# Batch 0's K in whole runs on 64 partitions, a third wide PSUM tile at the start, and attention-times-V visits in two parts, in an attention and gated-FFN kernel on one Trainium2 core

## The chip, the cores and the metric

The kernel runs on one core of one Trainium2 chip (trn2). The metric is the device time of one execution in microseconds (us); lower is better. Before the change the runs gave 460.41 us in the median of 3 (460.27 to 460.72).

## The reference

The attention has no softmax: scores are scaled, cut at zero, squared and divided by the sequence length. Its output, heads side by side, is the input of a gated feed-forward layer with an RMS norm ahead of it.

```python
# q, k, v: (8 batches, 12 heads, 448 positions, 64), float32
scores = (1 / sqrt(64)) * q @ k.T
attn   = maximum(scores, 0) ** 2 / 448
x      = heads_side_by_side(attn @ v)          # (8 * 448, 768)
xn     = x / sqrt(mean(x * x) + 1e-6) * rms_g
g, val = xn @ w_gate, xn @ w_val               # (3584, 1536) each
out    = (g * sigmoid(g) * val) @ w_out        # (3584, 768), float32
```

## The kernel before, in words

**The order of the work.** The program is written out by a planner that runs while the kernel is built (class `Planner`, L62). Every piece of work is an `Op` with a cost in us per engine, with operations it depends on, a rank, and sometimes a due time; the planner keeps a clock for each engine, picks the next piece and emits its instructions. No scheduler reorders them afterwards, so an engine executes in exactly this order, and waits on semaphores in order. The costs are numbers in the source (for example 0.14 + n x 0.000833 us for a ScalarE eviction of n columns, L413). When TensorE has nothing to do for 0.3 us or more in the plan, `fill` (L955) emits matmuls of ones and zeros that no one reads (L966).

**Data.** Q, K and V are loaded by GpSimd's DMA queue and turned into bf16 on the way (L255, L269). Positions are dealt to partitions in runs: a head's K of 448 x 64 stands on 128 partitions as 4 chunks of 64 columns on partitions 0 to 63 and 3 chunks on partitions 64 to 127, so each K load is two DMAs, and a `memset` (L240) fills the missing chunk. For batches 0 and 1 TensorE transposes Q and K (L369: per pair of heads 8 matmuls of 128 columns for K and 8 of 112 for Q; VectorE copies the result to `qkT`, L379); later batches use DMA transposes (L293). The loads stand on GpSimd's queue in the order Q and K of batch 0 in three steps of 2, 4 and 6 heads (with the identity matrix for the transposes made after the first), V, the gate and value weights in slices, batch 1, the output weights.

**Attention**, per group of four heads (j = 0, 2, 4): score matmuls (`scores_full` L425, `scores_half` L443 for batch 0, which is worked in two halves of 224 queries), the "rest" chunk, i.e. the last 64 keys of both head pairs (L461), each into a wide PSUM tile of two banks (there are two); ScalarE or VectorE cuts at zero (`relu`, L405, L407), VectorE squares in place (L411). Then the AV visit (`attend`, L538) multiplies by V with 28 matmuls on quarters of the array, 64 rows by 64 columns each, four side by side. Rows 0 to 63 and rows 64 to 127 of the array add into the same PSUM rows one after the other: first 16 matmuls (low half for one pair of heads, high half for the other), then, after a wait for those to land (an empty instruction with a dependency, L537), 12 with the halves exchanged. ScalarE evicts the visit (L565).

**Feed-forward.** For the norm, squares are summed by a matmul with ones (`norm_sums`, L769); ScalarE takes ln and exp (L607, L611), VectorE scales (L616). The projections form a stream (class `Stream`, L635): each group accumulates in one single PSUM bank (four of them) over its K chunks, first with rows 0 to 63 (half 0), then with rows 64 to 127 (half 1); a step emits half 0 of one group beside half 1 of another. Before its half 1 a group keeps `APART` = 2 slots of distance (L725) and an empty instruction that waits for half 0 (L737). Groups marked `quarters` are emitted with outputs of 64 rows (tile 64 x 64, two matmuls per half), others with 128 (tile 64 x 128); `step` (L685) uses quarters when one of the pair asks for it.

Of the kernel before, what the change touches and what calls it, by code (L numbers as in the profile page):

```python
# [8 lines left out]
FP32 = mybir.dt.float32  # L9
# [5 lines left out]
U = 7  # L15
UH = 4
# [3 lines left out]
class Op:  # L20


    def __init__(self, on, fn, deps=(), rank=0, pair=None, bank=False, ends=None, due=None, ring=None,
                 early=0.0, lean=()):
        self.on, self.ring, self.early = on, ring, early
        self.fn, self.deps, self.rank = fn, list(deps), rank
        self.pair, self.bank, self.ends, self.due = pair, bank, ends, due
        self.done = NEVER
        self.lean = dict(lean)
        self.ps = None  # L30
# [31 lines left out]
class Planner:  # L62


    def __init__(self, banks):
        self.free = {"PE": 0.0, "ACT": 0.0, "DVE": 0.0, "POOL": 0.0, "SP": 0.0}
        self.lists = {e: [] for e in self.free}
        self.users = [[] for _ in range(banks)]
        self.stream = None
        self.fill = None  # L70
        self.now = 0.0

# [12 lines left out]
    def start(self, op, e, t):  # L85
        for x in op.on:
            self.lists[x].remove(op)
        dur = op.on[e]() if callable(op.on[e]) else op.on[e]
        self.free[e] = t + dur
        op.engine, op.begun = e, t  # L90
        op.done = op.ends(t) if op.ends else t + dur + (0.06 if e != "PE" else 0.22)
        op.fn(op)
# [67 lines left out]
def kernel(  # L160
# [11 lines left out]
    nc = tc.nc  # L172
# [22 lines left out]
    pairs = [psum.tile([P, 2, 512], FP32, name=f"psS{i}", tag=f"psS{i}") for i in range(2)]  # L195
    banks = [psum.tile([P, 512], FP32, name=f"psP{i}", tag=f"psP{i}") for i in range(4)]
    wide = [Space(pairs[i], (2 * i, 2 * i + 1)) for i in range(2)]
    single = [Space(banks[i], (4 + i,)) for i in range(4)]
# [44 lines left out]
    def load(nm, b, h0=0, h1=H, deps=()):  # L243
        runs = nm == "v" or b < PE_T
        src = src_of[nm][b, h0:h1]
        if nm == "q":
            parts = [(slice(0, PC), PC, 0, NCH)]
        else:
            parts = [(slice(0, D), D, 0, UH), (slice(D, P), D, UH if nm == "k" else UH - 1, U)]
        ops = []  # L250
        for prt, n, u0, u1 in parts:
            kb = n * (u1 - u0) * D * 4 * (h1 - h0) / 1e3

            def whole(prt=prt, n=n, u0=u0, u1=u1):
                nc.gpsimd.dma_start(  # L255
                    out=stage(nm, b)[prt, h0:h1, : (u1 - u0) * D],
                    in_=src.rearrange("h (p u) d -> p h (u d)", p=n)[:, :, u0 * D : u1 * D],
                )

            if runs:  # L260
                ops.append(pool_dma(0.72, kb, 400.0, whole, deps))
                continue
            step = u1 - u0 if nm == "q" else 1
            for u in range(u0, u1, step):

                def piece(prt=prt, n=n, u=u, u0=u0, step=step):
                    to = stage(nm, b)[prt].rearrange("p u (h d) -> p u h d", d=D)
                    rows = src.rearrange("h (p u) d -> p u h d", p=n)
                    nc.gpsimd.dma_start(  # L269
                        out=to[:, u - u0 : u - u0 + step, h0:h1, :], in_=rows[:, u : u + step]  # L270
                    )

                ops.append(
                    pool_dma(2.3 if step > 1 else 0.75, kb * step / (u1 - u0), 280.0, piece, deps)
                )
        landed.setdefault((nm, b), {}).update({h: ops for h in range(h0, h1)})
# [4 lines left out]
    turned = {}  # L281
# [72 lines left out]

    def blocks():
        return ((0, D), (D, P)) if state["quarters"] else ((0, P),)
# [3 lines left out]
    def transposes(b, j):  # L360
        def fn(op):
# [3 lines left out]
            op.flat = flat  # L365
            for nm, n, w, at in (("k", P, UH, 0), ("q", PC, NCH, S)):
                for c in range(w):
# [19 lines left out]
        t = Op({"PE": 0.55}, fn, need, rank=-2, bank=True)  # L387
        copy = Op({"DVE": 0.63}, copy_fn, [t], rank=0)
# [7 lines left out]
    def evict_rect(t, n, key, group):  # L396
# [12 lines left out]
        def square(op):  # L409
# [3 lines left out]
        rl = add(Op({"ACT": 0.14 + n * 0.833e-3, "DVE": 0.13 + n * 1.042e-3}, relu,  # L413
                    [t] + r_ring.before, rank=2, lean={"DVE": 0.9}))
# [4 lines left out]
    def scores_full(b, j, c, due):  # L419
# [13 lines left out]
        return add(Op({"PE": 0.19}, fn, [Turned(b, j)], rank=-1, pair=wide, due=due,  # L433
                      ring=r_ring, early=0.4))

    def scores_half(b, lo, what, due):

        def fn(op):
# [10 lines left out]
            for i, (j, c) in enumerate(what):  # L449
# [4 lines left out]
                      pair=wide, due=due,  # L454
# [11 lines left out]

    def rest(b, j, lo, w, due):
        def fn(op):
            emit_rest(op.ps.tile, b, j, lo, w)
            rl, sq = evict_rect(op, 2 * w, (b, lo, j, "rest"), (b, lo, j))  # L470
            rests[b, lo, j] = (sq, rl)
            plan.take(op.ps.banks, [rl])

        return add(Op({"PE": 0.25}, fn, [Turned(b, j), Turned(b, j + 1)], rank=-1,
                      pair=wide, due=due,
                      ring=r_ring, early=0.4))
# [29 lines left out]
    sqs, rests, avs = {}, {}, {}  # L506
    xTs, accs, attended, normed = {}, {}, {}, {}

    def attend(b, j, lo, w, due):
# [9 lines left out]
        def fn(op):  # L519
            ps = op.ps.tile  # L520
# [9 lines left out]
            last = {}  # L530
            for first in (True, False):
                for step in range(UH - (not first)):
                    for prt, jj in ((low, 0), (high, 1)) if first else ((low, 1), (high, 0)):
                        r, u = order[prt][jj][step]
                        for hh in range(2):
                            if not first and step == 0:
                                tc.add_manual_dep(nc.tensor.nop().ins, last[jj, hh].name, behind)  # L537
                            mm = nc.tensor.matmul(  # L538
                                out=ps[hh * D : (hh + 1) * D, jj, :w],
                                lhsT=vb[prt, 2 * (j + jj) + hh, u * D : (u + 1) * D],  # L540
                                rhs=r[prt, hh, :],
                                start=(first and step == 0),
                                stop=(not first and step == UH - 2),
                            )
                            last[jj, hh] = mm.ins
            ev = add(Op({"ACT": 0.14 + 2 * w * 0.833e-3}, evict, [op], rank=1))
# [39 lines left out]
        for jj in range(2):  # L586
            for i in range(UH - 1):
                need.append(Later(sqs, (b, j + jj, i) if full else (b, lo, j + jj, i)))
        need += [o for h in range(2 * j, 2 * j + 4) for o in landed["v", b][h]]
        me = Op({"PE": (1.55 if full else 0.9)}, fn, need, rank=-1,  # L590
                pair=wide, due=due)
        avs[b, lo, j] = me
# [8 lines left out]
    def norm_scale(b, lo, w, g):  # L601
# [11 lines left out]
        def scale(kt):  # L613
# [8 lines left out]
        rt = add(Op({"ACT": lambda: 2 * (0.19 + w * 0.833e-3) + switch(LN_EXP)}, root, [g.end],  # L622
# [3 lines left out]
            add(Op({"DVE": 0.2 + w * 1.05e-3}, scale(kt), [rt], rank=-1)) for kt in range(KT)  # L626
# [8 lines left out]
    class Stream:  # L635


        APART = 2
# [37 lines left out]
        def step(self, t):  # L676
# [8 lines left out]
            state["quarters"] = any(g.quarters for _, g in pair)  # L685
# [7 lines left out]
            took = max(g.slot for _, g in pair)  # L693
# [14 lines left out]
    class Group:  # L708
# [15 lines left out]
        def ready_at(self, half):  # L724
            t = self.when + stream.APART * self.slot if self.last not in (None, half) else 0.0  # L725
# [42 lines left out]

    def norm_sums(b, lo, w):  # L769
        if (b, lo) == (0, 0):  # L770
            return Group(
                KT, w, lambda i: ones_bf[:], lambda i: x2_bf[:, i, :],
                lambda g: norm_scale(b, lo, w, g), "psSS",
                lambda i: [Later(squared, i // 2 * 2)], False,
            )
# [3 lines left out]
            w == S,  # L779
# [4 lines left out]
    def silu(b, fb, lo, w):  # L784
        def done(g):
# [6 lines left out]
            op = add(Op({"ACT": lambda: 0.14 + w * 0.833e-3 + switch(SILU)}, fn, [g.end], rank=0,  # L792
# [6 lines left out]
    def hidden(b, fb, lo, w):  # L799
        def done(g):  # L800
# [8 lines left out]
            op = add(Op({"DVE": 0.15 + w * 1.042e-3}, fn, need, rank=1))  # L809
# [42 lines left out]
    def store(i, t, o, w, g):  # L852
# [15 lines left out]
        op = add(Op({"ACT": 0.14 + w * 0.833e-3, "DVE": 0.13 + w * 1.042e-3}, fn, [g.end] + ([] if first else [osts[i, t][2]]),  # L868
# [51 lines left out]
    def attention_half(lo):  # L920
        for j in range(0, HP, 2):
# [6 lines left out]
            rest(0, j, lo, HS, now)  # L928
            attend(0, j, lo, HS, now)

    def attention_full(b):
# [4 lines left out]
        for j in range(0, HP, 2):  # L936
# [3 lines left out]
            base = {0: 0.0, 2: 0.06, 4: 0.46}[j]  # L940
            if j == 0:
                for m in range(6):
                    scores_full(b, m // 3, m % 3, at("o", 0.15 + m * 0.12) if b > 2 else at("gv", 0.0))
                rest(b, 0, 0, S, at("gv", 0.0))
                attend(b, 0, 0, S, at("gv", 0.06))
                continue
            rest(b, j, 0, S, at("gv", base))
            for m in range(6):
                scores_full(b, j + m // 3, m % 3, at("gv", base + 0.02 + m * 0.06))
            attend(b, j, 0, S, at("gv", base + 0.4))  # L950
# [21 lines left out]
    pool_ident = add(Op({"POOL": 0.6}, lambda op: masks.make_identity(nc, ident[:])))  # L972
    load("q", 0, 2, 6)
    load("k", 0, 2, 6)
    load("q", 0, 6, 12)
# [13 lines left out]
    stream.add([norm_sums(0, 0, HS)])  # L989
    for b in range(B):  # L990
        groups = ffn(b)
        if b == 0:
            stream.add(groups[:24])
            plan.run(lambda: (0, 0) in summed)
# [61 lines left out]
```

## Time and profile before

| what | value |
|---|---|
| median of 3 runs | 460.41 us (460.27 to 460.72) |
| the profiled execution | 460.52 us, its span 458.7 us |
| first transposes / first AV visit / first projection | 7.59 / 18.00 / 30.42 us |
| first transposes of batch 1 | 48.16 us |
| start of the last matmul | 453.27 us |
| gate and value matmuls (L739, 64 x 448) | 349 ns each, four side by side |
| relu on ScalarE (L407), 128 x 896 | 908 ns |
| DMA moved | 44.75 MB, mean 98 GB/s |

How the views are read: the page has a line for each engine with its busy time and share of the span; PE is TensorE's matmuls, PEld its weight loads, which run beside them, DVE is VectorE, ACT ScalarE, POOL GpSimd. "PEclk" gives the granted TensorE clock in 40 slices, in tenths (9 is 90% or more). The chain of waits follows the work that ended last back to what released each step; "issue" is time for which nothing in the profile accounts. Rows of groups have the line, the engine, the operation, output<-input and the count, then busy time and mean length, then idle time before them and what ended it. A matmul's length in the records holds its pipeline, so the pace is read from starts.

### The profile page before, as it was taken

What the parts mean: (1) busy time and instruction counts of PE and PEld (TensorE: products, weight loads), DVE (VectorE), ACT (ScalarE), POOL (GpSimd) and SP (SyncE); (2) the same over time, 40 slices, a digit from 0 to 9 for tenths busy, and PEclk for the clock granted to TensorE, in tenths of its full rate; (3) what the DMA queues carried; (4) which work ended last, traced back from release to release, by engine and by line L of the source; (5) the groups of instructions that cost most, each with busy time, mean ns of one, the idle gap of its engine ahead of it and who ended that gap; (6) DMA issues with size and microseconds to landing.
All of it is one profiled execution on the core that took longest, in us unless ns stands there. A gap on an engine that the chain in (4) does not pass through costs nothing.

```text
span 458.7 us, 17067 instructions
## 1 busy us (share of the span) xinstructions
PE 447.9 (98%) x7829; PEld 338.9 (74%) x7829; DVE 243.6 (53%) x405; ACT 268.7 (59%) x394; POOL 78.4 (17%) x99
## 2 busy tenths in 40 slices
PE   8999999999899999999999999999999999999995
PEld 7668777777459777677769777677768777689974
DVE  1777786475645446636655347546655357522200
ACT  1685986485557565767647656667647657522221
POOL 8522711661061000700052000100000000000000
PEclk9999999999999999999999999999999999999999
DMA  9999999999969921994049920951002200021013
GB/s 103 198 204 200 203 181 150 139 185 160 136 78 168 137 74 27 142 195 59 1 62 171 143 80 20 143 102 37 3 2 64 65 16 3 1 79 29 1 37 103
DMA packets 130855, 44.75 MB, mean 98 GB/s; under 512 B 103008, under 2 KB 127200, under 8 KB 130784
## 3 DMA queue, kind: packets, MB, share of 16 engines
q0 software_dynamic: 91728, 24.39, 56.8%
q1 hardware_dynamic: 39056, 19.28, 24.4%
q8 instruction: 61, 1.00, 0.9%
q14 instruction: 10, 0.08, 0.1%
HBM read 48.76 MB, written 11.01 MB: 130 GB/s over the span
## 4 chain that ended last, share of the span: by engine, by line
PE 94%; DMA 2%; ACT 1%; POOL 1%; issue 1%; DVE 0%; ACTq 0%; POOLq 0%
PE psP L739 76%; PE psS L538 9%; PE psS L425 6%; DMA kb<-in_k_dram 2%; PE psS L461 1%; PE psP L966 1%; PE psS L443 1%; PE psP L369 1%; POOL kb L255 1%; ACT L343 1%; POOL qb L255 0%; ACT xT L565 0%; ACT r L407 0%; DVE xn L569 0%; ACT sil L789 0%
## 5 line engine op out<-in xcount | busy, mean ns | idle before, releaser
L739 PE MATMUL psP<-xn,wg_sb 64*64 64x448 bf16 (+1 forms) x2304 | 212.5, 338 | 1.6 <-issue 1.6
L739 PE MATMUL psP<-xn,wv_sb 64*64 64x448 bf16 (+1 forms) x2304 | 197.6, 338 | 0.1
L407 ACT ACTIVATE r<-psS 128x896 bf16<-128x896 f32 (+1 forms) x168 | 146.7, 908 | 55.5 <-PE psS L425 41.9
L739 PE MATMUL psP<-wo_sb,hT 64*128 64x384 bf16 (+1 forms) x1519 | 146.9, 324 | 0.0
L739 PEld LDWEIGHTS <-wg_sb 64*64 64x64 bf16 (+1 forms) x2304 | 123.7, 105 | 24.8 <-issue 3.8
L739 PEld LDWEIGHTS <-wv_sb 64*64 64x64 bf16 (+1 forms) x2304 | 121.2, 105 | 23.6 <-issue 4.0
L411 DVE TENSOR_TENSOR r<-r 128x896 bf16<-128x896 bf16 (+1 forms) x171 | 102.1, 613 | 67.6 <-ACT r L407 67.2
L739 PEld LDWEIGHTS <-hT 64*128 64x128 bf16 (+1 forms) x1519 | 103.1, 97 | 26.4 <-issue 9.7
L803 DVE TENSOR_TENSOR hT<-sil,psP 128x448 bf16<-128x448 bf16 (+1 forms) x108 | 61.2, 566 | 38.4 <-PE psP L739 37.9
L789 ACT ACTIVATE sil<-psP 128x448 bf16<-128x448 f32 (+1 forms) x108 | 54.0, 500 | 36.9 <-PE psP L739 36.3
L565 ACT ACTIVATE xT<-psS 128x896 bf16<-128x896 f32 (+1 forms) x27 | 22.5, 834 | 50.9 <-PE psS L538 50.9
L425 PE MATMUL psS<-qkT 64*64 64x448 bf16 (+1 forms) x412 | 48.2, 352 | 0.2 <-ACT r L407 0.2
L860 ACT COPY ost<-psP 128x384 f32<-128x384 f32 x55 | 26.4, 480 | 32.9 <-PE psP L739 32.7
L538 PE MATMUL psS<-r,vb 64*64 64x448 bf16 (+1 forms) x756 | 43.7, 333 | 1.9 <-PE psS L538 0.3
L255 POOL DMA_DIRECT2D vb<-in_v_dram x20 | 14.3, 728 | 166.2 <-PE psS L538 89.4
L616 DVE SCALAR_TENSOR_TENSOR xn<-xT,g_sb,rstd 128x448 bf16<-128x448 bf16 (+1 forms) x54 | 30.2, 627 | 15.2 <-ACT rstd L611 15.2
L269 POOL DMA_DIRECT2D kb<-in_k_dram x42 | 33.3, 1050 | 16.1 <-DMA wo_sb<-in_moe_w_out_dram 8.8
L538 PEld LDWEIGHTS <-vb 64*64 64x64 bf16 x756 | 22.2, 106 | 18.4 <-PE psS L538 11.2
L575 DVE TENSOR_TENSOR x<-xT 128x896 f32<-128x896 bf16 (+1 forms) x16 | 16.5, 1033 | 33.2 <-ACT xT L565 33.2
L425 PEld LDWEIGHTS <-qkT 64*64 64x64 bf16 (+1 forms) x412 | 20.3, 103 | 7.1 <-issue 2.9
L343 ACT ACT_TABLE_LOAD x18 | 23.1, 1283 | 1.0 <-PEq L1040 0.7
L575 DVE TENSOR_TENSOR acc<-xT 128x896 f32<-128x896 bf16 (+1 forms) x8 | 8.3, 1033 | 22.8 <-ACT xT L565 22.8
(37 smaller groups left out, 155.9 us busy)
## 6 DMA issues: line engine op xcount, KB each, us to landing
vb<-in_v_dram POOLq DMA_DIRECT2D x12, 384.0 KB, 7.5
kb<-in_k_dram POOLq DMA_DIRECT2D x43, 96.0 KB, 12.0
qb<-in_q_dram POOLq DMA_DIRECT2D x6, 672.0 KB, 15.4
out_dram<-ost SPq DMA_DIRECT2D x8, 336.0 KB, 3.1
wg_sb<-in_moe_w_gate_dram POOLq DMA_DIRECT2D x4, 576.0 KB, 15.2
wv_sb<-in_moe_w_val_dram POOLq DMA_DIRECT2D x4, 576.0 KB, 17.2
wo_sb<-in_moe_w_out_dram POOLq DMA_DIRECT2D x2, 1152.0 KB, 14.0
out_dram<-ost SPq DMA_DIRECT2D x8, 288.0 KB, 2.7
```

What stands on the lines that cost most here:

```text
L269: nc.gpsimd.dma_start(out=to[:, u - u0 : u - u0 + step, h0:h1, :], in_=rows[:, u : u + step])
L343: nc.scalar.add_instruction(mybir.InstLoadActFuncSet(name=name, act_func_set_id=n, ins=[], outs=[]))
L407: nc.scalar.activation(out=op.view, in_=src, func=ACT.Relu)
L411: eng.tensor_tensor(out=rl.view, in0=rl.view, in1=rl.view, op=ALU.mult)
L425: nc.tensor.matmul(out=ps[m0:m1, hh, :S], lhsT=qkT[b][prt, j, 0, c * P + m0 : c * P + m1], rhs=qkT[b][prt, j, 1, :], start=True, stop=True,)
L538: mm = nc.tensor.matmul(out=ps[hh * D : (hh + 1) * D, jj, :w], lhsT=vb[prt, 2 * (j + jj) + hh, u * D : (u + 1) * D], rhs=r[prt, hh, :], st ...
L575: nc.vector.tensor_tensor(out=dst, in0=x, in1=x, op=ALU.mult)
L616: nc.vector.scalar_tensor_tensor(out=xns[b][:, kt, lo : lo + w], in0=xTs[b][:, kt, lo : lo + w], scalar=g_sb[:, kt : kt + 1], in1=rstd[:, ...
L739: mm = nc.tensor.matmul(out=self.ps[m0:m1, : self.w], lhsT=self.lhsT(i)[prt, m0:m1], rhs=self.rhs(i)[prt], start=(half == 0 and i == 0), s ...
L789: nc.scalar.activation(out=s[:, :w], in_=g.ps[:, :w], func=ACT.Silu)
L803: nc.vector.tensor_tensor(out=hT[:, fb, o : o + w], in0=sil[b, fb, lo][1][:, :w], in1=g.ps[:, :w], op=ALU.mult,)
L860: nc.scalar.copy(out=to, in_=g.ps[:, :w])
```

## The change

Eight things change, all in the writing of the instruction list:

1. Batch 0's K is loaded with 7 positions a partition on 64 partitions, one DMA a load, into a part of the output weights' tile that is not yet used; its transposes are 14 matmuls of 64 columns on quarters. The identity is made after two loads of each.
2. Until the sums of batch 0's first half are done, four single banks are two, and a third wide tile stands in their place.
3. An AV visit becomes two operations, and the next group's rest chunk depends on the first of them having been issued, with rank -4 (ahead of the second, rank -3).
4. The planner knows a form for each TensorE operation and adds 0.12 us where it changes; the stream keeps quarters while a quarter group is open.
5. The norm's sums don't ask for quarters; those of the first half of batch 0 become three operations with whole 128-row matmuls.
6. A group's second half follows after max(slot, 0.2) us instead of two slots.
7. The planned costs and latencies of ScalarE, VectorE and TensorE operations are changed.
8. For batch 1, transposes use one single bank, and the order of rest and scores within a group is changed.

```diff
@@ Planner.start @@
         dur = op.on[e]() if callable(op.on[e]) else op.on[e]
+        if e == "PE":
+            dur += self.changed(op.form() if callable(op.form) else op.form)
         self.free[e] = t + dur
-        op.engine, op.begun = e, t
-        op.done = op.ends(t) if op.ends else t + dur + (0.06 if e != "PE" else 0.22)
+        op.engine, op.begun, op.left = e, t, t + dur
+        op.done = op.ends(t) if op.ends else t + dur + {"ACT": 0.17, "DVE": 0.13, "PE": 0.22}.get(e, 0.1)
...
+    wide = [bank_pair(psum, i) for i in range(2)]
+    single = [bank(psum, i) for i in (4, 5)]
+    head = tc.tile_pool(name="psum_head", bufs=1, space=bass.MemoryType.PSUM)
+    wide.append(bank_pair(head.__enter__(), 3))
+
+    def end_head():
+
+        wide.pop()
+        head.__exit__(None, None, None)
+        pool = ctx.enter_context(tc.tile_pool(name="psum_rest", bufs=1, space=bass.MemoryType.PSUM))
+        single.extend(bank(pool, i) for i in (6, 7))
@@ load @@
+        if (nm, b) == ("k", 0):
+
+            def runs_of_seven():
+                nc.gpsimd.dma_start(
+                    out=wo_sb[:D, h0:h1, :S], in_=src.rearrange("h (p u) d -> p h (u d)", p=D)
+                )
@@ transposes @@
+            for u in range(U if b == 0 else 0):
+                at = u * P if u < UH else (u - UH) * P + D
+                for hh in range(2):
+                    nc.tensor.transpose(
+                        out=flat[hh * D : (hh + 1) * D, at : at + D],
+                        in_=wo_sb[:D, 2 * j + hh, u * D : (u + 1) * D],
+                        identity=ident[:D, :D],
+                    )
@@ evict_rect @@
-        rl = add(Op({"ACT": 0.14 + n * 0.833e-3, "DVE": 0.13 + n * 1.042e-3}, relu,
-                    [t] + r_ring.before, rank=2, lean={"DVE": 0.9}))
+        rl = add(Op({"ACT": 0.05 + n * 0.833e-3, "DVE": 0.07 + n * 1.042e-3}, relu,
+                    [t] + r_ring.before, rank=2, lean={"DVE": 0.5 if key[:2] == (0, 0) else 3.0 if key[0] == 0 else 0.9}))
@@ rest @@
-        return add(Op({"PE": 0.25}, fn, [Turned(b, j), Turned(b, j + 1)], rank=-1,
-                      pair=wide, due=due,
-                      ring=r_ring, early=0.4))
+        need = [Turned(b, j), Turned(b, j + 1)] + ([Issued(ones[b, lo, j - 2])] if j else [])
+        return add(Op({"PE": 0.0025 + w / 2400.0}, fn, need, rank=-4 if j else -1,
+                      pair=wide, due=due, form="q", ring=r_ring, early=0.4))
@@ attend @@
+        def begin(op):
+            plan.take(op.ps.banks, [me])
+            products(True, op.ps.tile)
+
+        def fn(op):
+            op.ps = one.ps
+            products(False, op.ps.tile)
...
-        me = Op({"PE": (1.55 if full else 0.9)}, fn, need, rank=-1,
-                pair=wide, due=due)
-        avs[b, lo, j] = me
+        slot = w / 2400.0 + 0.0025
+        one = Op({"PE": UH * slot}, begin, need, rank=-1, pair=wide, due=due, form="q")
+        me = Op({"PE": (UH - 1) * slot}, fn, [one], rank=-3, form="q")
+        avs[b, lo, j], ones[b, lo, j] = me, one
+        add(one)
         return add(me)
@@ Stream.step, Group.ready_at @@
-            state["quarters"] = any(g.quarters for _, g in pair)
+            state["quarters"] = any(g.quarters for _, g in pair) or any(
+                g.quarters and g.count[0] for g in self.open
+            )
...
-            took = max(g.slot for _, g in pair)
+            took = max(g.slot for _, g in pair) + plan.changed(form())
...
-            t = self.when + stream.APART * self.slot if self.last not in (None, half) else 0.0
+            t = self.when + max(self.slot, 0.2) if self.last not in (None, half) else 0.0
@@ norm_sums (the first half of batch 0 has a class Sums of its own) @@
             lambda g: norm_scale(b, lo, w, g), "psSS", lambda i: [Later(summed, (b, lo))],
-            w == S,
+            False,
@@ the loads @@
     load("k", 0, 0, 2)
-    pool_ident = add(Op({"POOL": 0.6}, lambda op: masks.make_identity(nc, ident[:])))
     load("q", 0, 2, 6)
     load("k", 0, 2, 6)
+    made["ident"] = add(Op({"POOL": 0.6}, lambda op: masks.make_identity(nc, ident[:])))
```

## Prediction

> **What bounds the kernel now.** I read the page first (engine shares, clock, chain), then the chain of waits around one attention visit, the group row of that line, the timeline around changes of tile form, and the chain of the first 16 us.
>
> ```profile
> span 458.7 us, 17067 instructions
> PE 447.9 (98%) x7829; PEld 338.9 (74%) x7829; DVE 243.6 (53%) x405; ACT 268.7 (59%) x394; POOL 78.4 (17%) x99
> ...
> PEclk9999999999999999999999999999999999999999
> ...
> PE 94%; DMA 2%; ACT 1%; POOL 1%; issue 1%; DVE 0%; ACTq 0%; POOLq 0%
> ```
>
> TensorE is busy or holds the chain throughout, at full clock, while VectorE and ScalarE have 40% to spare. So the time is the length of TensorE's own instruction list, and the question is how much of that list is no work. The chain of waits from 181 to 187 us (start, length, what):
>
> ```profile
> 180.99 1.51 PE psP L739 x32
> 182.51 0.81 PE psS L538 x16
> 183.32 0.01 issue
> 183.33 0.79 PE psS L538 x12
> ```
>
> 32 gate/value matmuls of 448 columns, four side by side on quarters of the array, are 8 slots in 1.51 us: 0.189 us a slot. The attention-times-V visit (L538) has 28 matmuls, 7 slots, which should take 1.32 us; it takes 0.81 + 0.01 + 0.79 = 1.61. So 0.29 us a visit is a wait in its middle, where the second products (3 slots) may only start when the first (4 slots) have landed in the same PSUM rows. The group row of the line and a timeline around 13.5 us (start, length, engine, line, what):
>
> ```profile
> L538 PEld LDWEIGHTS <-vb 64*64 64x64 bf16 x756 | 22.2, 106 | 18.4 <-PE psS L538 11.2
> ```
> ```profile
> 12.59 0.94 PE L966 MATMUL psP<-busy_bf,ones_bf 128*128 128x224 bf16 x8
> 13.48 0.29 PE L461 MATMUL psS<-qkT 64*64 64x224 bf16 x4
> 13.70 0.36 PE L966 MATMUL psP<-busy_bf,ones_bf 128*128 128x224 bf16 x2
> ```
>
> The weight loads of L538 stood 11.2 us behind L538 itself. In the timeline, 8 fills of 224 columns are 8 x 0.096 = 0.77 us, yet the next form (64*64) starts 0.89 after the first of them; its one slot of 0.096 takes 0.22 until the form goes back. Each change of form costs **0.12 us**. The third loss is the head:
>
> ```profile
> 6.57 0.61 POOL kb L255
> 7.17 7.13 DMA kb<-in_k_dram
> 14.30 0.04 issue
> 14.35 1.46 PE psP L369 x48
> ```
>
> The third part of batch 0's K lands at 14.30; the first gate/value matmul follows at 30.42 (timeline), and 79 of the 120 fills (matmuls that do no work) stand between the first transposes (7.59) and it.
>
> **The change, part by part.** The built order of both kernels is known, so instructions can be counted; only waits are open.
>
> *AV visits split.* In the built order two slots (the next group's rest chunk and a gate/value slot, or two gate/value slots) stand between the 16 and the 12 of every visit of full width but the first, which has two transposes there, and the two beside half-width projections, which have more. Inside a visit now, the fifth slot starts 0.45 us after the fourth (0.189 of work, 0.26 of wait). With two slots between it is 0.57 after: no wait is left. 21 full visits x 0.29 = **-6.0 us**. Behind the waiting matmuls stands all of TensorE's list, so nothing else becomes late in exchange; the eviction of a visit (L565) comes 0.38 later, and the wide tile with it. The six half-width visits lose 6 x 0.28 = 1.7; of them one keeps its wait, one has a single slot of 0.096 in the gap (0.14 stays), four lose it for two further changes of form each, which the next part counts: **-1.3**.
>
> *Changes of form.* Counted in the built orders: 117 before, 86 after. Up to batch 1's first transposes they rise from 41 to 50, from there on they fall from 76 to 36 (per later batch from 8 to 2, since quarters are kept while such a group is open and the sum-of-squares group no longer asks for them). 31 x 0.12 = **-3.7**. At a change both halves of the array must be empty, and laid end to end by slots without waits the two lists differ by 3.7: 2.2 of that are 23 fewer fills (0.096 each), **-1.5** the rest, mostly halves that stood idle until the other had ended.
>
> [...]
>
> *New half-to-half waits.* The stream now lets a group's second half follow after one slot or 0.2 us, before after two. 224-column visits show 0.096 + 0.23 us needed from the last first-half matmul's start, 448-column ones 0.189 + 0.26; 384 columns show no such wait before, so I bound it by these two and take 0.25. In the built order 16 out-projection groups stand 0.32 apart and lack 0.095 each (1.5), the norm sums, six gate/value groups and some visits about 0.4 more: **+1.9** (bounds 0, if the wait is shorter there, and +3, if the 36 groups that stand 0.42 apart wait too).
>
> *Head.* By counts from the first transposes to the first gate/value matmul: fills 79 to 60 (-1.8), score visits 14 to 11 (3 x 0.19 = -0.6), one rest less (-0.1), K's transposes 14 of 64 columns (0.2 us) for 8 of 128 (0.22) (0), the norm sums in whole form without their half-to-half waits (-0.9), the waits of the three visits 0.85 to 0.4, one or two more changes (+0.2), K's wait of 0.28 + 0.15 at 14.3 gone: 22.83 becomes **18.6**, and with 4 fewer fills ahead of the first transposes (7.59 to 7.2) the projection starts at 25.8 instead of 30.4. ScalarE is the engine beside it (by the starts of its rows some 11 us of work in 18); the third wide tile lets it run three evictions behind. The single tiles that it takes away feed nothing there but transposes and fills.
>
> *To batch 1's transposes.* Before 17.74 us with 233 projection matmuls; after 258 (+1.2), 3 scores and a rest more (+0.7), 7 changes more (+0.8), visit waits -0.7: 19.7, so **45.5** instead of 48.16. Those transposes need batch 1's K: heads 0 to 5 landed at 47.9 (issued by GpSimd at 30.2, 17.7 us to landing). Nothing but the queue's order holds that, since DMA moves 198 to 204 GB/s from 11 to 57 us (page). What moves it is the start: GpSimd issues K in three DMAs instead of six, so the last K part goes out 3 x 0.61 = 1.8 us sooner; at the most the queue also loses its slack (1.4 MB of Q and K at 200 GB/s from 2.8 us would end at 9.7 and land near 10.1, 4.2 sooner). Between 1.8 and 4.2 I take 3.0, the middle: K of batch 1 at 44.9, just ahead of TensorE. At 1.8 it costs 0.6, at 0 2.4. The identity, now issued after two loads of each, is done by some 4.6 us, and the first transposes need it at 7.2; past it move one Q and one K load.
>
> [...] Each of the six K loads before already writes 64 partitions, and 11 to 14 us shows 184 to 202 GB/s with them. [...]
>
> *From there to the end.* Before 405.1 us (48.16 to 453.27, the last matmul's start). Visits -6.0, 40 changes fewer -4.8, new waits +1.9, 25 projection matmuls already done -1.2, idle halves -1.3; and a single stall of 1.6 us (with nothing shown that released it, at 123.2 in the timeline) may or may not be met again: -0.8. 405.1 becomes **392.9**. The planner's ScalarE and VectorE costs now are nearer to the starts in the trace (relus 0.81 apart), so I expect evictions on time.
>
> *Sum.* -0.4 (fills ahead) -4.2 (head) +2.0 (to batch 1) -12.2 = -14.8; I give back 0.6 for small waits of the new order: **-14.2**. The profiled execution took 460.52 (span 458.7 and 1.8 around it): 446.3. The median of the runs is 460.41, 0.1 less, so I say 446.2.
>
> **Rivals.**
> 1. *The transfers don't come sooner* (or K lands late on 64 partitions). Then TensorE stands before batch 1's transposes for the 2.4 us above: 448.6, and up to 3 more if K lands later than now; about 449. For it: DMA is saturated from 14 to 57 us. Against: the queue was underfed from 2 to 7 us (10 to 152 GB/s). Chance 0.16.
> 2. *The visits' wait moves.* With the rest chunk pulled between two visits, its eviction stands ahead of the visit's own, and the next score waits for a wide tile, of which two are left after the head. If each of the 21 full visits so returns its 0.29: 446.2 + 6 = 452. Against: ScalarE is 59% busy. Chance 0.13.
> 3. *Slower: evictions become the bound.* The planner now counts 0.80 us for a wide relu, 0.09 less than before; the records last 0.908. If the real pace were the record's length, each of the 168 evictions (L407) would free its tile 0.11 late and TensorE, in order, would stand: +18, 464. It decides from 0.085 us an eviction (14.2 / 168). Against: four relus stand in 2.97 us on ScalarE's timeline, closer than their lengths. Chance 0.04.
> 4. *The split does nothing* (the wait for the landing is ordered elsewhere): 446.2 + 7.3 = 453.5. Chance 0.02.
> 5. Better still (no new half waits, no stall): 442 to 444. Chance 0.05.
>
> **How the numbers follow.** The forecast has the remaining 0.60, with 443.5 to 449 as its own range. Cases 1 and 2 reach to 452, so the range is 442.5 to 452. A difference under 0.2% can't be told from none here. All cases but 3 are faster: 0.95; within 0.2% 0.01, slower 0.04.
>
> **What would show it.** Right: in the chain of waits the 12 of a visit follow other matmuls, and L538's idle row falls from 11.2 to about 2; the first gate/value matmul near 26, batch 1's first transposes near 45.5, and 361.77 to the last matmul (91.5 before) shorter by about 2. Wrong: score matmuls waiting for ScalarE, a DMA ahead of L369's successor, or out-projection rows with gaps of more than 0.1 us.

## The result and the profile after

The changed kernel took 455.42 us (median of 4 runs, 453.62 to 456.05), the kernel before 460.57 beside it (460.27 to 461.36): a ratio of 0.988, 95% interval 0.985 to 0.991. The direction was right, but 446.2 was forecast and the range ended at 452.0: of 14.2 us, 5.2 came. The profiled execution took 453.62, 7.3 over the 446.3 that the prediction's sum gave for it.

The page of the changed kernel (span; busy time of each engine, share, instructions; granted clock in 40 slices; the engines' shares of the chain that ended last):

```profile
span 451.9 us, 16996 instructions
...
PE 440.2 (97%) x7805; PEld 327.5 (72%) x7805; DVE 241.7 (53%) x403; ACT 268.8 (59%) x395; POOL 76.8 (17%) x96
...
PEclk9999999999899999999999999999999999999998
...
PE 88%; DMA 9%; issue 1%; POOL 1%; ACT 0%; ACTq 0%; POOLq 0%
```

TensorE still bounds the kernel, but a DMA now stands in the chain with 9% (2% before), and in the eleventh slice the clock was not full. In the changed kernel's source the projections stand at L802 (L739 before), the visits at L590 (L538), the scores at L468 (L425), the rest chunk at L504 (L461) and the transposes at L411 (L369), batch 0's K at L403. Three group rows, the first of the kernel before (busy, mean ns of one, then the idle time before them and what ended most of it):

```profile
L739 PE MATMUL psP<-xn,wg_sb 64*64 64x448 bf16 (+1 forms) x2304 | 212.5, 338 | 1.6 <-issue 1.6
...
L802 PE MATMUL psP<-xn,wv_sb 64*64 64x448 bf16 (+1 forms) x2304 | 204.6, 340 | 3.1 <-issue 3.1
...
L590 PEld LDWEIGHTS <-vb 64*64 64x64 bf16 x756 | 24.5, 106 | 10.0 <-issue 1.8
```

The 11.2 us that the AV line's weight loads stood behind their own matmuls are gone (the greatest reason left has 1.8), as predicted. The gate/value matmuls, however, now wait 3.1 us for nothing that the profile shows; before it was 1.6. The chain of waits around one visit shows the split at work (start, length, what):

```profile
108.68 0.76 PE psS L590 x16
109.44 0.19 PE psS L504 x4
109.63 0.19 PE psP L802 x4
109.82 0.57 PE psS L590 x12
```

16 and 12 matmuls now take 0.76 and 0.57, 1.33 us in all where the visit took 1.61, and two slots of other work stand between. So that step did what it should. The chain shows how; what the split is worth is measured below. Where the time went shows when TensorE's starts are set against the prediction. Visits are counted from 0, half-width ones too; A9 is the start of visit 9. The last column is the kernel "held" of the experiments, whose TensorE list is that of the changed kernel, matmul for matmul:

| start, us | before | predicted | after | held |
|---|---|---|---|---|
| batch 0's first transposes | 7.59 | 7.2 | 6.72 | 7.63 |
| first gate/value matmul | 30.42 | 25.8 | 26.64 | 26.92 |
| batch 1's first transposes | 48.16 | 45.5 | 46.77 | 46.76 |
| A9 | 102.58 | | 97.65 | 97.92 |
| A12 | 153.46 | | 151.19 | 147.44 |
| last matmul | 453.27 | 438.4 | 446.36 | 442.86 |

Up to A9 4.9 us are won; from A9 to A12 2.7 of them are lost again (50.88 before, 53.54 after, while held takes 49.52 for the same matmuls); behind A12 4.65 are won. The chain in the stretch:

```profile
117.02 2.13 PE psP L802 x39
119.16 1.71 issue
120.87 0.82 PE psP L802 x6
121.69 0.37 PE psS L468 x4
122.06 3.52 PE psP L802 x48
```

TensorE stands 1.71 us for no shown reason, and 1.2 us later 48 matmuls take 3.52 us, where the chain elsewhere has 48 in 2.33. The windows of the same stretch show why the second happens (the DMA share adds up the time of packets over that of 16 engines and passes 1 where packets overlap; it serves for comparison only):

```profile
core 0: us, PE busy (x) PEld busy (x) DVE busy (x) ACT busy (x) POOL busy (x), PEclk, DMA share, GB/s
118.00:120.00 2.00, 1.16 (x19) 0.49 (x18) 1.69 (x3) 0.85 (x2) 0.00 (x0) 1.00 1.97 81
120.00:122.00 2.00, 1.13 (x16) 0.94 (x19) 0.00 (x0) 0.28 (x1) 0.00 (x0) 0.76 2.58 129
122.00:124.00 2.00, 2.00 (x27) 1.11 (x23) 0.00 (x0) 1.08 (x2) 0.00 (x0) 0.50 3.78 131
```

The clock falls to half for 3.4 us after the stall (0.50 from 121.05 to 124.46). Two smaller stalls stand at 105.5 and 112.5, one at 209.9. The kernel before had a large one, the one that the prediction booked with -0.8, as something that "may or may not be met again"; the clock stayed full behind it (1.00 in every window from 122 to 130 us):

```profile
123.22 0.37 PE L739 MATMUL psP<-xn,wg_sb 64*64 64x448 bf16 x1 [1.59 <-issue]
```

### The profile page after: what moved, and what is told of

It reads as the page before. It is cut to its first block, busy times and chain, and to the rows that moved or that the text cites. A ratio compares the mean times of both kernels' runs of the same rounds, so it can differ in the third digit from the quotient of the medians.

```text
span 451.9 us, 16996 instructions
## 1 busy us (share of the span) xinstructions
PE 440.2 (97%) x7805; PEld 327.5 (72%) x7805; DVE 241.7 (53%) x403; ACT 268.8 (59%) x395; POOL 76.8 (17%) x96
## 4 chain that ended last, share of the span: by engine, by line
PE 88%; DMA 9%; issue 1%; POOL 1%; ACT 0%; ACTq 0%; POOLq 0%
PE psP L802 74%; PE psS L590 6%; PE psS L468 6%; DMA kb<-in_k_dram 4%; DMA wv_sb<-in_moe_w_val_dram 4%; DMA wo_sb<-in_k_dram 2%; PE psS L504 1%; PE psP L411 1%; POOL qb L286 0%; POOL wo_sb L270 0%; ACT ost L941 0%; POOL ident masks.py:199 0%; POOL ident masks.py:197 0%; ACTq L941 0%; POOLq L1126 0%
## 5 line engine op out<-in xcount | busy, mean ns | idle before, releaser
L802 PE MATMUL psP<-xn,wg_sb 64*64 64x448 bf16 (+1 forms) x2304 | 222.1, 340 | 0.0
L802 PE MATMUL psP<-xn,wv_sb 64*64 64x448 bf16 (+1 forms) x2304 | 204.6, 340 | 3.1 <-issue 3.1
L450 ACT ACTIVATE r<-psS 128x896 bf16<-128x896 f32 (+1 forms) x169 | 148.3, 913 | 47.3 <-PE psS L468 25.3
L802 PEld LDWEIGHTS <-wg_sb 64*64 64x64 bf16 (+1 forms) x2304 | 123.5, 105 | 39.8 <-PE psP L802 9.1
L802 PE MATMUL psP<-wo_sb,hT 64*128 64x384 bf16 (+1 forms) x1502 | 139.5, 323 | 0.0
L802 PEld LDWEIGHTS <-wv_sb 64*64 64x64 bf16 (+1 forms) x2304 | 118.0, 105 | 29.0 <-issue 4.3
L802 PEld LDWEIGHTS <-hT 64*128 64x128 bf16 (+1 forms) x1502 | 101.8, 97 | 22.7 <-issue 2.8
L468 PE MATMUL psS<-qkT 64*64 64x448 bf16 (+1 forms) x412 | 50.5, 352 | 0.0
L590 PE MATMUL psS<-r,vb 64*64 64x448 bf16 (+1 forms) x756 | 45.8, 331 | 0.1
L590 PEld LDWEIGHTS <-vb 64*64 64x64 bf16 x756 | 24.5, 106 | 10.0 <-issue 1.8
L468 PEld LDWEIGHTS <-qkT 64*64 64x64 bf16 (+1 forms) x412 | 21.7, 104 | 5.9
L637 DVE TENSOR_TENSOR acc<-acc,x 128x896 f32<-128x896 f32 (+1 forms) x16 | 16.5, 1033 | 0.6
## 6 DMA issues: line engine op xcount, KB each, us to landing
kb<-in_k_dram POOLq DMA_DIRECT2D x42, 96.0 KB, 14.2
```

What stands on the lines that cost most here:

```text
L450: nc.scalar.activation(out=op.view, in_=src, func=ACT.Relu)
L468: nc.tensor.matmul(out=ps[m0:m1, hh, :S], lhsT=qkT[b][prt, j, 0, c * P + m0 : c * P + m1], rhs=qkT[b][prt, j, 1, :], start=True, stop=True,)
L590: mm = nc.tensor.matmul(out=ps[hh * D : (hh + 1) * D, jj, :w], lhsT=vb[prt, 2 * (j + jj) + hh, u * D : (u + 1) * D], rhs=r[prt, hh, :], st ...
L802: mm = nc.tensor.matmul(out=self.ps[m0:m1, : self.w], lhsT=self.lhsT(i)[prt, m0:m1], rhs=self.rhs(i)[prt], start=(half == 0 and i == 0), s ...
```

## The experiments

**What the stalls are.** One count was made on the traces alone: TensorE's instructions (matmuls, weight loads and the few semaphore instructions that the profile lists) are numbered in the order of their starts, and for five numbers the table gives the largest gap in ns between two starts there. An ordinary gap at these places is 30 to 180.

| kernel | 3266 | 3522 | 3778 | 4034 | 4290 |
|---|---|---|---|---|---|
| before | 150 | 92 | 402 | 1941 | 162 |
| before_v_first | 150 | 92 | 152 | 150 | 146 |
| after | 152 | 709 | 1120 | 2058 | 178 |
| late | 151 | 1047 | 1120 | 2332 | 177 |
| whole | 632 | 609 | 1207 | 1943 | 146 |
| forms | 29 | 1164 | 1243 | 2491 | 1242 |
| apart2 | 404 | 1244 | 1095 | 1966 | 1668 |
| v_first | 180 | 985 | 297 | 156 | 177 |
| held | 439 | 436 | 120 | 90 | 374 |
| vf_apart2 | 150 | 30 | 230 | 92 | 93 |

The columns are 256 instructions apart. In kernels with different lists the large gaps fall on the same numbers, whatever the instruction there does, and later ones (7106 at 209.9 us in after) lie a multiple of 256 further. The five kernels not in the table agree: vf_whole, vf_forms and vf_kold have a gap of 618, 1068 and 1067 at 3522 (vf_forms another of 420 at 3778), vf_wide2 one of 1138 at 3778, and held_apart2 one of 874 at 9410, which is 21 x 256 behind 4034. One 16-KB packet of the DMA queue "instruction" comes for each such step (61 in the changed kernel's page, and TensorE's 15,632 listed instructions are 61 x 256 and 16 more). The reading that fits all this is that TensorE waits there for its own next block of instructions. In the changed kernel the packets for 3522, 3778 and 4034 begin when TensorE is 180, 204 and 214 instructions into the block before, where from 155 to 187 us, with little DMA (a share of 0.37 against 1.71 from 105 to 121), most begin within 60. The packets themselves take 0.97, 0.95 and 0.89 us, no longer than others (0.89 to 1.89 from 60 to 215 us): it is their start that is late, and the stalls end 2.3 to 3.3 us after it.

What moves there in the changed kernel: from 98 to 121 us the DMA transposes of batch 3's Q and K (256-byte packets); beside them up to 108 us batch 3's V (512-byte packets), and from 106 us on batch 4's Q and K (128-byte packets; issued from 97.1, but they stand behind V). So the gap at 3522, at 105 us, has only V beside the transposes; those at 3778 and 4034 have Q and K.

**v_first** and **before_v_first**: in the changed kernel and in the one before, from batch 4 on V is loaded ahead of Q and K. V's buffer comes free late, so that Q and K wait behind it on GpSimd's queue. TensorE's list is not touched.

```
+            if b >= 2:
+                load("v", b + 2, deps=last)
+                seen = last
             load("q", b + 2, deps=seen)
             load("k", b + 2, deps=seen)
-            load("v", b + 2, deps=last)
+            if b < 2:
+                load("v", b + 2, deps=last)
```

> The changed kernel with one edit: from batch 4 on, V is loaded ahead of Q and K, so that Q and K of batches 4 to 7 wait on GpSimd's queue behind V, which waits for an attention visit some 20 us later. TensorE's list is the same, instruction for instruction. Theory A (the stalls of 0.4, 0.8 and 1.7 us at 105, 112 and 119 us, and the half clock after the last, are TensorE waiting for its own instructions, which come by DMA and stand behind the small packets of batch 4's Q and K beside batch 3's transposes): the stalls go, the clock stays at 1.0 from 121 to 124 us, and the time falls by 3 to 5 us to 449 to 451. Theory B (they belong to this place of the list: an unlisted wait or a change of form): the same stalls stay at the same matmuls, time within 1 us of the changed kernel. Theory C (DMA traffic matters, but moves with the loads): the stalls go from 100 to 125 and come again some 20 us later, time within 2 us.

> The same edit in the kernel before, TensorE's list unchanged. Theory A: its one stall of 1.6 us at 121 to 123 us goes, 458 to 459. Theory B: it stays, 460.4. Theory C: a stall of about that size elsewhere.

Measured: 450.02 (448.66 to 450.92; 0.976 of before, 0.973 to 0.978) and 458.62 (457.79 to 459.13; 0.994, 0.992 to 0.996), beside 460.93 for the kernel before. TensorE's waits in v_first (us, times, longest):

```profile
PE psP L802 <- issue: 0.6, 1, 0.6
```

5.4 us come off the changed kernel by its median (3.3 in the profiled executions) and 2.3 off the one before; both times lie inside theory A's spans, and the gap at 4034 is gone in both. Theory A's other half did not hold for all: the gap at 3522 stays in v_first (985 ns), where V moves beside the transposes as before. With the loads moved in both, the change is worth 8.6 us and not 5.2.

**late** and **held** ask whether it helps that V goes first, or that the small packets move apart from the transposes. late keeps the order and gives the loads one more condition in the planner; held makes the wait a real one, on GpSimd, for the last transpose of the batch before (kept in `moved`).

```
# late
+            after = list(turned[b + 1]) if b >= PE_T else []
-            load("q", b + 2, deps=seen)
+            load("q", b + 2, deps=seen + after)
...
# held
+                def hold(op, b=b):
+                    tc.add_manual_dep(nc.gpsimd.nop().ins, moved[b + 1].ins.name, behind)
+                seen = [add(Op({"POOL": 0.1}, hold, seen + turned[b + 1]))]
             load("q", b + 2, deps=seen)
```

> The changed kernel with the order of the loads as it is (Q, K, V), but from batch 4 on all three wait until the DMA transposes of the batch before have ended. TensorE's list is the same. In the traces so far every stall of TensorE near 105 to 130 us stands at one of its instructions 3266, 3522, 3778, 4034 or 4290 (matmuls and weight loads counted), 256 apart, whatever kernel and whatever the instruction is, and 16-KB packets of the instruction queue begin 2.3 to 3.3 us before its end. Theory (the fetch of the next 256 instructions is late while the transposes and the 128-byte packets of Q and K move together): nothing of Q and K or V now lies beside the transposes, so no gap over 0.3 us at these numbers, not even the one of 1.0 that v_first kept beside V's 512-byte packets: 449.2 to 450. Rival (that V goes first is what helps, not that the small packets move apart): 453.6 to 456 as the changed kernel.

> The changed kernel with one more wait: GpSimd issues batch 4's first Q load only when the last DMA transpose of batch 3 has landed (later batches waited for theirs already). The order of the loads and TensorE's list are those of the changed kernel. 'late' did not tell: its condition stood only in the planner's estimate, which held it for met, and its Q load was issued at 97.6 instead of 97.1 with the landing at 122.9 as before. Theory (128-byte packets of Q and K beside the transposes delay the fetch of TensorE's next 256 instructions): the stalls at its instructions 3522, 3778 and 4034 shrink to the one of up to 1.0 that v_first kept beside V's packets, 449.5 to 450.5. Rival (V going first was what helped): 453.6 to 456.

late took 454.83 (453.13 to 455.78; 0.986, 0.984 to 0.989) and tells nothing between the two: the planner's conditions only order the loads by estimates, the first Q load was issued at 97.6 instead of 97.1, and the stalls are all there. held took 451.17 (450.12 to 452.93; 0.978, 0.976 to 0.981), 0.7 above the theory's span and 2.4 below the rival's. Its Q load (time of the issue on GpSimd in ns, shortest, median, longest; first and last start in us) and what GpSimd waited for before that line:

```profile
L300 POOL DMA_DIRECT2D qb<-in_q_dram x1: 2272/2272/2272, 113.6 to 113.6; - x1
...
  DMA qkT<-kb: 16.9, 1
```

```profile
PE psP L802 <- issue: 0.4, 1, 0.4
```

Q now starts at 113.6, after the transposes, the order is as it was, and the stalls at 3778 and 4034 are gone. So the overlap of Q and K with the transposes makes these two fetches late. It does not make all of them late: at 3266 and 3522 gaps of 0.44 stay, and one of 0.75 at 7106. No run moved V away from the transposes, so the cause of the gap at 3522 is not tested. One thing speaks against the load on the DMA engines alone: from 120 to 125 us, with Q and K by themselves, held shows a higher DMA share (2.57) than the changed kernel from 116 to 120 (1.66 and 1.97), and its only gap there is 0.37 (held first, then the changed kernel):

```profile
120.00:125.00 5.00, 4.97 (x105) 2.86 (x100) 2.31 (x4) 2.19 (x4) 1.15 (x2) 1.00 2.57 154
...
116.00:118.00 2.00, 2.00 (x43) 1.37 (x36) 0.25 (x1) 1.31 (x3) 0.00 (x0) 1.00 1.66 161
118.00:120.00 2.00, 1.16 (x19) 0.49 (x18) 1.69 (x3) 0.85 (x2) 0.00 (x0) 1.00 1.97 81
```

Which part of the path the fetch stands in is open.

**whole, vf_whole**: all 28 matmuls of a visit in one piece, in the changed kernel and on top of v_first (`products(True, ...)` and `products(False, ...)` both in `begin`).

> The changed kernel with the 28 matmuls of each AV visit in one piece again (rest chunks still right behind a visit). My theory: each of 21 full visits gets its 0.29 us back, 6 us, and the half-width ones 1.3 less the changes of form that the split made there (76 changes in place of 86): laid end to end the list is 5.5 us longer; 460 to 461 if DMA stalls stay as they are. Rival (the split's gain was given back by the evictions behind it): under 3 us.

> The changed kernel with V loaded ahead of Q and K from batch 4 on (v_first, 450.0 us), and each AV visit's 28 matmuls in one piece. Question: is the split worth its sum of matmul slots once TensorE's stalls of 100 to 125 us are out of both kernels, or only the 3.3 us that 'whole' lost against the changed kernel? Theory (slots): the list of matmuls is 5.45 us longer by the slots of the prediction's rows, 3.0 of it before batch 1's first transposes, where the landing of K covers part; so 454.5 to 455.5. Rival (the wait only moves): 453.3 or less.

**forms, vf_forms**: without the planner's price on a change of form, without holding on to quarters, the sums in quarters again (`return 0.0`; the `or any(g.quarters ...)` dropped; `w == S` put back).

> The changed kernel without its steps on the tile form: no planned price for a change, quarters only where a pair asks for them, later norm sums in quarters again: 118 changes of form in place of 86. My theory, at 0.12 us a change and the halves idle at them: the list laid end to end is 6.5 us longer, 460 to 462. Rival (a change is hidden, since the other half of the array still works): under 2 us.

> v_first without the price on changes of form, without holding on to quarters while a group is open in them, and with the norm sums in quarters again: 118 changes of form instead of 86, and 13 more fills. Theory (slots): the list is 6.5 us longer, 3.3 of it before batch 1's first transposes, so 455.5 to 456.6. Rival (as 'forms' against the changed kernel, 3.1): 453.1; in that case half of what the slots say is covered by the landing of batch 1's K.

Measured: whole 458.76 (456.69 to 461.07), forms 458.55 (457.96 to 459.51): 3.3 and 3.1 above the changed kernel, both with stalls of 2 us and both below what was expected from the slots (460 at the least). vf_whole 454.96 (454.45 to 455.93) and vf_forms 454.23 (453.79 to 454.77): 4.9 and 4.2 above v_first, with gaps left (0.6 in vf_whole, 1.1 and 0.4 in vf_forms) much as v_first has them (1.0 and 0.3). So without the great stalls the split is worth 4.9 (5.45 by the slots, inside the theory's span) and the handling of forms 4.2 (6.5 by the slots, between theory and rival). Of the forms' shortfall 1.7 stands before batch 1's transposes: they start 1.6 later in vf_forms than in v_first (49.42 and 47.83), where the slots said 3.3. Part of that is v_first's own late head (its gate/value matmuls start at 27.99, those of vf_forms at 27.23); the rest is open. On the kernel with stalls the two look a quarter to a third smaller (3.3 and 3.1).

**vf_kold, vf_wide2**: v_first with batch 0's K loaded and turned as before; v_first without the third wide tile.

> v_first with batch 0's K loaded and turned as before (128 partitions in packets of 128 and 64 columns, eight transposes of 128 rows). Prediction on record had K's new form free the queue 3.0 us earlier; the trace of the changed kernel shows a lead of 1.3. Theory: first transposes at about 7.6 instead of 6.7, batch 1's K landed near 48 instead of 46.9 and its transposes with it (+1.1), while the list of matmuls is 2.1 us longer up to there (covered by that landing) and 1.75 shorter behind it; sum 449.4, so the new form of K is worth nothing or costs half a microsecond. Rival (the prediction's lead of 3.0 on both sides of that): 451.3 to 452.

> v_first without the third wide PSUM tile in the first half of batch 0 (two wide tiles and four single ones throughout). Theory: the list is 2.7 us longer (119 fills instead of 97), 1.1 of it before batch 1's first transposes where K's landing at 46.9 covers it, so 451.6. Rival (nothing is covered, the scores wait for evictions as well): 452.7 or more. Second rival: the tile is worth nothing, 450.0.

vf_kold took 450.01 (449.03 to 451.38): with the medians equal (0.5 apart in the profiled executions) the new form of K shows no gain; the time is 0.6 above the theory and below the rival. vf_wide2 took 451.04 (449.89 to 453.25): 1.0 by the medians, 0.3 in the profiled executions, between the first theory's 1.6 and nothing. With runs up to 3.4 apart that does not settle what the tile is worth.

**vf_apart2, held_apart2, apart2**: the second half of a group two slots behind the first again, on v_first, on held and on the changed kernel.

```
-            t = self.when + max(self.slot, 0.2) if self.last not in (None, half) else 0.0
+            t = self.when + 2 * self.slot if self.last not in (None, half) else 0.0
```

> v_first with the second half of a group allowed two slots after the first, as before the change, instead of one. Theory (slots): the list is 1.2 us longer, since the halves that stand idle cost more than the waits for the landing that go (12 of them in out-projections); 451.2. Rival: the new half-to-half waits are larger than the prediction's 1.9 (the last stage of the changed kernel stands 1.0 us over its slots), so that without them 448.5 to 449.5 would come out.

> The same with the second half of a group two slots behind the first, as before the change. vf_apart2 ran 1.5 us below v_first, but most of that stands in one stage (47.96 instead of 49.50 from the ninth to the twelfth attention visit, where v_first had a fetch stall of 1.0); behind it the two differ by 0.4 only. Theory (the distance of one slot is worth nothing: what it saves in idle halves, 0.7 us of slots behind the twelfth visit, the waits for the landing take back): 0.3 to 0.6 below 'held' where neither or both meet a stall. Rival (the distance of one slot costs): 1.5 or more below 'held', also where the stages show no stall.

> The changed kernel with only the distance of a group's second half put back to two slots; the loads are those of the changed kernel, so batch 4's Q and K move beside batch 3's transposes again. Theory (the distance of one slot is worth about nothing, and what delays the fetches is the small packets): the stalls at TensorE's instructions 3778 and 4034 are there, A9 to A12 some 52 to 54 us, and the time 453 to 455, that is 0.4 to 2.2 below the changed kernel. Rival (the order of matmuls with one slot is what meets the late fetches): no stall over 0.4, A9 to A12 about 48, 448.5 to 450.

They took 448.54 (447.26 to 449.39), 448.99 (448.05 to 451.11) and 452.26 (450.19 to 453.14): 1.5, 2.2 and 3.2 below their partners, so the first theory (451.2) fell, and the rivals of the first two runs were nearer. In the third the stalls stay, as its theory said, though the time is 0.7 below the theory's span. So the distance of one slot is not what makes the stalls, which apart2 has in full:

```profile
PE psP L802 <- issue: 4.6, 4, 1.6
```

From A12 to the last matmul, where none of these three has a stall, the profiled executions give 294.1 for two slots (vf_apart2, apart2) and 294.5 for one (v_first): one slot costs 1.3 up to visit 24 (202.79 and 204.05) and saves 0.9 behind it (91.3 and 90.5). The profiled executions of apart2 and the changed kernel lie 0.5 apart (453.14, 453.62), their medians 3.2. What makes the difference of 1.5 to 3.2 in the medians stays open beyond these 0.4. vf_apart2 is the fastest version found: 0.973 of before (0.971 to 0.976), with no gap over 0.23 us at the counted places.

## Why the prediction was wrong

**The step that failed most** is the last term of "From there to the end": "a single stall of 1.6 us (with nothing shown that released it, at 123.2 in the timeline) may or may not be met again: -0.8". By the reading of the counts above it was a fetch of instructions, bound to where transposes and loads lie, and the changed kernel comes to these places with the same loads around it (its Q load is issued at 97.09, before at 97.06). In the changed kernel the gaps at 3522, 3778, 4034 and 7106, less 0.15 each, are 3.9 us. The half clock behind the gap at 4034 cost another 1.6: matmul for matmul the changed kernel stands 2.51 behind held just after the stall and 4.13 some 50 matmuls later. Before, the gaps were 2.0 and the clock stayed full. So the term is +3.5 in place of -0.8, which is 4.3 of the 7.3 us. Why the same loads cost the changed kernel more than the kernel before is open. held, with 1.4 us left at these places, ran 3.5 below the changed kernel in the profiled executions and 4.3 by the medians. No rival had more or longer stalls, and so the range was too narrow.

**K's lead** (to batch 1's transposes: 45.5 forecast, 46.77 measured, +1.3). "What moves it is the start" was wrong. Batch 0's last K part was issued 1.8 sooner, as the text said, and did land sooner, 13.00 instead of 14.30, and V's last part too (17.01, 18.35). But the first weight slice landed at 21.28 in place of 21.23: the same bytes had moved by then, K only earlier among them. A DMA now stands ahead of L411 in the chain, one of the signs of being wrong that the text named. Batch 1's K (heads 0 to 5) landed at 46.64 instead of 47.91, a lead of 1.3 and not 3.0, between the 1.8 and the 0 for which the text had prices and which it did not take. The chain of the changed kernel:

```profile
13.29 16.46 DMA wv_sb<-in_moe_w_val_dram
29.74 0.28 issue
30.03 16.61 DMA kb<-in_k_dram
46.64 0.14 issue
46.77 0.61 PE psP L411 x16
```

It shows what the prediction missed: from the 12th load to the 28th (9.5 to 45.1 us) GpSimd issues each 0.28 or 0.29 us after the load eight places before has landed (the 14th load at 13.29 after the 6th, K's last part, at 13.00; the 22nd, batch 1's K, at 30.03 after the 14th, a weight slice, at 29.74), so there a start moves only as that landing does. Rival 1 (the transfers don't come sooner) was right in kind, at half its 2.4 us. vf_kold then shows no gain from the form of K in all: with the new form (v_first) batch 1's transposes start 2.5 us sooner (47.83 and 50.32), and from there to the last matmul it takes 1.9 longer (395.19 and 393.27).

**The head** came 0.8 later (26.64 for 25.8), though the transposes began 0.5 sooner: K's wait, which the sum had as gone, is still there with 0.8 us, and the norm sums wait 0.7 for VectorE. Kernels with the same list and loads start the gate between 26.6 and 28.0, by how late K lands and by the clock behind that wait (K's last part at 13.00 us and full clock in the changed kernel, 26.64; at 13.78 and half clock, 0.50 from 16 to 18 us, in v_first, 27.99). Rival 1 adds up to 3 us in case K on 64 partitions lands later than before, a term that no run shows: from 10 to 14 us the changed kernel moved 186 and 197 GB/s, the one before 184 and 193, and K's last part landed 1.3 us sooner.

**What was right.** Visits and forms, in kind (the chain, and vf_whole and vf_forms); in size the visits' 7.3 stands against the 4.9 of vf_whole, whose list has ten changes of form less in exchange (10 x 0.12 = 1.2), and the 3.7 and 1.5 of the forms against the 4.2 of vf_forms. Right were also TensorE as the bound, and that no score waits for ScalarE (rival 3). The net 0.4 of the halves' distance (+1.9 and -1.5) came out in size from A12 on; that is partly luck, since it covers other work than those terms did, and the medians of the two-slot kernels lie 1.5 to 3.2 lower. The sign "361.77 to the last matmul shorter by about 2" came out at 1.0 (91.50 to 90.48). With two slots it takes 91.3, so the new waits between halves alone do not explain it; that microsecond is open. Together: 4.3 for the stalls, 1.3 for K's lead, 1.0 in the last stage, and 0.7 not taken apart. The median lies another 1.8 above the profiled execution, the shortest of the changed kernel's runs; whether longer stalls make that is not shown, since one execution was profiled.

## What to carry to other kernels

A wait that the profile gives no releaser is a finding and not noise: count the instruction it stands at, and see whether others stand a fixed number away, before giving it half its size. In this kernel, bound by a long unrolled list, transfers that nobody waits for cost time (moving them gave 5.4 us by the medians in v_first, 4.3 in held), by all that the counts show by delaying the engine's own instructions; look at when loads start, not only at when they must land. A lead won at the head of a saturated queue can be lost on the way: here, at 186 to 205 GB/s from 10 to 24 us, 1.8 us at the issue were 1.3 at K's landing and nothing at the first weight slice, for which as many bytes lay ahead as before.

## What the runs showed of the hardware

The granted clock fell to half after waits shorter than the stall at 120 us. In v_first TensorE waited 1.1 us for K up to 13.8; the windows that follow (columns as above):

```profile
14.00:16.00 2.00, 1.93 (x64) 1.66 (x60) 1.38 (x3) 0.00 (x0) 1.64 (x2) 0.80 1.47 194
16.00:18.00 2.00, 2.00 (x23) 1.28 (x20) 2.00 (x4) 1.11 (x2) 1.64 (x2) 0.50 1.35 200
18.00:20.00 2.00, 1.94 (x41) 1.15 (x39) 1.96 (x4) 0.71 (x2) 0.82 (x1) 0.85 1.33 209
```

The clock stood at half from some 15 to 19 us, and held_apart2 shows the same after a wait of 1.1 at 9.7 (0.50 from 12 to 14 us). But waits of 1.6 in the kernel before and 2.1 in forms were followed by full clock (1.00; 1.7 in the changed kernel by 0.50), so length alone does not decide.
